# The first microseconds of a planned kernel: who loads the small table, who clears the state matrices, when the function table is loaded, and how long the zero products are

## The chip, the cores and the metric

The kernel runs on one core of one Trainium2 chip. A core has TensorE (PE, matmuls, with a separate record PEld for loading the stationary operand), VectorE (DVE), ScalarE (ACT), GpSimd (POOL) and SyncE (SP), which only issues transfers; 16 DMA engines move the data. The engines run their own instruction streams and meet at semaphores. The metric is device time in microseconds. Before the change it was 640.88 us, the median of three runs (640.83 to 641.22).

## The reference

A decay attention (linear attention with a decay per head) is followed by a feed-forward layer with a squared ReLU. All inputs are float32: q, k, v of 4 x 8 x 768 x 64 (batch, heads, positions, head size), one decay `lam` per head between 0.97 and 0.99, weights `w_in` 512 x 2048 and `w_out` 2048 x 512.

```python
for b in range(nb):                                  # blocks of 64 positions
    intra = np.einsum('bhic,bhjc->bhij', qb, kb) * Dmask[None]      # lam ** (i - j), i >= j
    intra = np.einsum('bhij,bhjd->bhid', intra, vb)
    inter = np.einsum('bhid,bhde->bhie', qb * lam_pow[None], kv_state)
    out[:, :, sl] = intra + inter
    kv_state = lam_block[None, :, None, None] * kv_state + np.einsum('bhsd,bhse->bhde', kb_dec, vb)
x = attn_out.transpose(0, 2, 1, 3).reshape(B * S, H * D)            # 3072 x 512
h = np.maximum(x @ w_in, 0.0)
return h * h @ w_out
```

## The kernel before

**The work.** Positions are cut into chunks of 128, six for each of the four batches; eight tiles of three chunks (384 rows) go through the feed-forward layer, which takes 16 steps per tile, one per 128 columns of `w_in`. A step is twelve matmuls into `h` (L507: the weights and the activations are each split into a high and a low part, and three of the four products are kept), the squared ReLU on ScalarE and VectorE, and nine matmuls into three output banks (L513, L514, L516). The attention of a chunk is done in two units of four heads. Nine chunks, those needed first, go through `unit_plain` (L302) in plain float32, the other fifteen through `unit_split` with operands in two parts.

**A plain unit.** SyncE loads one operand tile `pnt` of 512 KB (L311; four buffers). TensorE makes the scores of the four heads (L317); VectorE multiplies them with the mask (L322). ScalarE weights the values with the decay powers `wdec` (L328, four instructions). TensorE makes the state's update from the weighted values (L340), ScalarE scales it with `lc` into the next state (L356; for plain successors into the diagonal blocks of `diag`, whose other blocks must be zero), and TensorE adds up the values (L366 for the old state, L369 for the scores). VectorE multiplies with `rdec` (L372), and ScalarE and VectorE split the result into the two parts of `x` (L375, L376). `rdec` is made once: `wdec` is spread out by VectorE (L254), turned by TensorE with a flipped identity (L251) and scaled by VectorE (L258).

**The tables.** `start_tables` (L221) loads the 6 KB `lamx` (the decays, in two layouts) through SyncE's queue, clears `zero` (the matrix that the zero products read, which later serves as an output buffer), makes the position and chunk exponents, the flipped identity and the mask, clears the four `diag` buffers on POOL (L233), and raises the decays to their powers on POOL (L235 for `wdec`, L236 for `lc`). The function table of ScalarE is not loaded by a line of its own: it stands before the first ACTIVATE that the program has, that of L328.

**The order.** The order of all instructions on all engines is written out by a planner. Each operation has an engine, an estimated duration in us, a key (lower goes first), operations it depends on, and buffers. `order` (L77) keeps one clock per engine and takes, again and again, the operation that can start earliest; among those of an engine that can start at about the same time the lowest key wins. The estimate for a finished load is its duration plus 2.0 us, for POOL's work its duration plus 0.12. A matmul planned before `PE_SLOW` counts double. Where TensorE has a gap in the plan before `FILL_END` (45 us) and an output bank is free, the planner puts in products of zeros (`filler`, L238) that take `FILL` us each (double before `PE_SLOW`). The instructions are then emitted in that order; on the chip each engine runs its own in this order and waits where its data or its buffer isn't ready. The planner's clock has no other influence on the chip. The first operation, `start_tables`, is planned on POOL with 1.2 us; loads of tiles and weights depend on it in the plan (`o_start`), and the weighting of values depends on `o_pow`, 3.0 us on POOL behind it.

Of the kernel before, what the change touches and what calls it, by code (L numbers as in the profile page):

```python
# [19 lines left out]
P = 128  # L20
# [21 lines left out]
PLAIN, SPLIT = CHUNKS[:N_PLAIN], CHUNKS[N_PLAIN:]  # L42
# [17 lines left out]
class Plan:  # L60
# [13 lines left out]
        self.ops.append(o)  # L74
        return o

    def order(self, pe_slow, fill):  # L77

        need, out = {}, {}
        for o in self.ops:  # L80
            both = set(map(id, o.deps)) | set(map(id, o.after))
            need[id(o)] = len(both)
            for d in both:
                out.setdefault(d, []).append(o)
        ready = {e: [o for o in self.ops if o.eng == e and not need[id(o)]] for e in self.LAT}
        free = dict.fromkeys(self.LAT, 0.0)
        slots = {k: [(0.0, i) for i in range(n)] for k, n in self.slots.items()}
        done, filled, early = [], 0, sum(o.early is True for o in self.ops)
        while any(ready.values()):
            best = None  # L90
            for e, ops in ready.items():
                can = []
                for o in ops:
                    t = max([free[e]] + [d.end + d.lat for d in o.deps])
                    want = {}
                    for b in o.bufs:
                        if b.slot is None:
                            want[b.kind] = want.get(b.kind, 0) + 1
                    ok = o.early is not False or not early
                    for k, n in want.items():  # L100
                        if len(slots[k]) < n:
                            ok = False
                            break
                        t = max(t, sorted(slots[k])[n - 1][0] + 0.15)
                    if ok:
                        can.append((t, o))
                if not can:
                    continue
                soon = max(free[e], min(t for t, _ in can)) + 0.05
                t, o = min(((t, o) for t, o in can if t <= soon), key=lambda x: (x[1].key, x[0]))  # L110
                if best is None or t < best[0]:
                    best = (t, o)
            assert best is not None, "no operation can get its buffers"
            t, o = best
            if o.eng == "PE" and t < fill:

                while free["PE"] + (long := FILL * (2.0 if free["PE"] < pe_slow else 1.0)) < t:
                    bank = min(slots["bank"], default=(t, 0))
                    if bank[0] > free["PE"]:
                        break  # L120
                    done.append(Op("PE", long, 0, lambda i=bank[1]: self.filler(i), [], [], [], 0, None))
                    done[-1].start, done[-1].end = free["PE"], free["PE"] + long
                    free["PE"] += long
                    filled += 1
            dur = o.dur * (2.0 if o.eng == "PE" and t < pe_slow else 1.0)
            o.start, o.end = t, t + dur
            free[o.eng] = o.end
            for b in o.bufs:
                if b.slot is None:
                    slots[b.kind].sort()  # L130
                    b.slot = slots[b.kind].pop(0)[1]
                b.left -= 1
                b.end = max(b.end, o.end + o.lat)
                if not b.left:
                    slots[b.kind].append((b.end, b.slot))
            ready[o.eng].remove(o)
            done.append(o)
            early -= o.early is True
            for d in out.get(id(o), ()):
                need[id(d)] -= 1  # L140
                if not need[id(d)]:
                    ready[d.eng].append(d)
        assert len(done) - filled == len(self.ops), "operations need each other"
        return done
# [10 lines left out]

FIRST, SLOW_STEP, LAG, BEGIN2, SECOND, STEP, PE_SLOW, FILL_END, FILL = 18.0, 6.5, 16, 9.0, 1.5, 4.8, 7.0, 45.0, 0.43

BEHIND = 12  # L160

# [4 lines left out]
def kernel(ctx: ExitStack, tc: tile.TileContext, pn, pk, lamx, w, out):  # L166
    nc = tc.nc
# [3 lines left out]
    plan = Plan()  # L171
# [12 lines left out]
    tiles = {}  # L184
# [10 lines left out]
    flip, zero = tiles["g"][-1][:, 0:P], tiles["ob"][-1]  # L195
    lam, ej, ec = (tiles["g"][-1][:, P + 16 * i:P + 16 * i + n] for i, n in enumerate((H + NP, H, NP)))
# [20 lines left out]
    def at(b):  # L217
        return tiles[b.kind][b.slot]


    def start_tables():  # L221
        nc.sync.dma_start(out=lam, in_=lamx)
        nc.vector.memset(zero, 0.0)
        nc.gpsimd.iota(ej, pattern=[[0, H]], base=MID, channel_multiplier=-1, allow_small_or_imprecise_dtypes=True)
        nc.vector.memset(ec, float(C))

        nc.vector.memset(flip, 1.0)
        nc.vector.memset(mask, 1.0)
        nc.gpsimd.affine_select(out=flip, in_=flip, pattern=[[1, P]], compare_op=ALU.is_equal, fill=0.0, base=1 - P, channel_multiplier=1)
        nc.gpsimd.affine_select(out=mask, in_=mask, pattern=[[1, P]], compare_op=ALU.is_ge, fill=0.0, base=0, channel_multiplier=-1)  # L230

        for d in tiles["diag0"] + tiles["diag1"]:
            nc.gpsimd.memset(d, 0.0)  # L233

        nc.gpsimd.tensor_tensor(out=wdec, in0=lam[:, 0:H], in1=ej, op=ALU.pow)  # L235
        nc.gpsimd.tensor_tensor(out=lc, in0=lam[:, H:H + NP], in1=ec, op=ALU.pow)  # L236

    def filler(i):  # L238
        nc.tensor.matmul(tiles["bank"][i][:, 0:2 * P], zero[:, 0:P], zero[:, P:3 * P], start=True, stop=True)

    plan.filler = filler

    o_start = plan.op("POOL", 1.2, -99, start_tables, early=True)


# [3 lines left out]
    def turned():  # L249
# [9 lines left out]
        out=rdec, in0=at(rps).rearrange("p (n i) -> p n i", n=NP), in1=lam[:, H:H + NP].unsqueeze(2).broadcast_to([P, NP, C]), op=ALU.mult),  # L259
# [33 lines left out]
    def in_turn(name, o):  # L293

        if turn.get(name):
            o.after.append(turn[name])
        turn[name] = o
        return o
# [3 lines left out]
    def unit_plain(b, c, q, x, col, key, behind=None):  # L302

        prs = slice(2 * q, 2 * q + 2)
        t, s1, vd, xr = Buf("pnt"), Buf("s1"), Buf("vd"), Buf("xr")

        def add(eng, dur, dk, fn, deps, bufs, name=None):
            o = plan.op(eng, dur, key + dk, fn, deps, bufs, early=True)
            return in_turn(name, o) if name else o

        load = add("SP", 1.7, -8, lambda: nc.sync.dma_start(out=at(t), in_=pn[PLAIN.index((b, c)), q]), [o_start, behind], [t], "load")  # L311
        sc = [Buf("bank"), Buf("bank")]

        def scores():
# [5 lines left out]
        if (b, c, q) == (0, 0, 0):  # L320
            o_turned.after.append(o)
        so = [add("DVE", 0.36, 0, lambda h=h: nc.vector.tensor_tensor(  # L322
            out=at(s1).rearrange("p (n h) i -> p n h i", h=2)[:, :, h], in0=at(sc[h])[:, 0:2 * C].rearrange("p (n i) -> p n i", n=2),
# [38 lines left out]
        def values():  # L362
# [10 lines left out]
            out=at(xr), in0=at(y)[:, 0:2 * C].rearrange("p (n i) -> p n i", n=2), in1=rdec[:, prs], op=ALU.mult), [o, o_rdec], [y, xr], "xr")  # L373
# [3 lines left out]
            out=at(x)[1][:, prs, cs], in0=at(xr), in1=at(x)[0][:, prs, cs], op=ALU.subtract), [oh], [xr, x])  # L377
# [175 lines left out]
    begin = [FIRST, FIRST + LAG * SLOW_STEP]  # L553
# [5 lines left out]
    for f in range(NF):  # L559
        t = FIRST + f * SLOW_STEP  # L560
        ws.append((weights(f, 0, t - 7), weights(f, 1, t - 2)))
    for ti, cs in enumerate(TILES):
        x = Buf("x")
        ready = []
        n = len(cs) * NQ
        for j, (b, c) in enumerate(cs):
            for q in range(NQ):
                i = j * NQ + q
                if ti == 0:
                    ready += unit_plain(b, c, q, x, j * C, i * 1.5)  # L570
                elif ti == 1:
                    ready += unit_plain(b, c, q, x, j * C, BEGIN2 + i * SECOND)
                elif (b, c) in PLAIN:
                    ready += unit_plain(b, c, q, x, j * C, begin[ti - 1] + (1 + i / n * 11) * per[ti - 1], steps[0, BEHIND])
                else:

                    f0 = 0.5 if ti > 2 else 1.0
                    ready += unit_split(b, c, q, x, j * C, begin[ti - 1] + (f0 + i / n * (13 - f0)) * per[ti - 1], 4.0)
        os_ = [Buf("bank") for _ in cs]
        for f in range(NF):  # L580
            ffn(ti, f, x, ready, ws[f], os_, begin[ti] + f * per[ti])


    done = plan.order(PE_SLOW, FILL_END)
    opened = False
    n_early = sum(o.early is True for o in done)
    with tc.manual_schedule():
# [50 lines left out]
```

## Time and profile before

| | us |
|---|---|
| median of three runs | 640.88 |
| lowest and highest | 640.83, 641.22 |
| the profiled execution | 641.31 |
| its span, first to last instruction | 639.6 |
| TensorE busy in the span | 631.4 |
| VectorE busy | 469.4 |
| ScalarE busy | 372.1 |
| POOL busy | 5.5 |
| matmuls that ended the chain: L507, share of the span | 41% |
| the same for L513, L514 and L516, each | 14% |

Times in the trace are counted from the start of the span. "PE L317 x8" is eight records: each matmul of plain float32 operands stands there twice, so that the four matmuls of the scores make eight records. A row such as "5.50 0.71 PE L317 MATMUL ..." gives start, length, engine, line, operation, output and inputs, and in brackets how long the engine had been idle and what released it. SPq is SyncE's own stream of transfer issues. TensorE was granted its full clock share through the whole profile. A matmul's end is modelled, so starts are surer than lengths.

### The profile page before, as it was taken

Reading aid. Unit: us, or ns where it says so; the run is one execution under the profiler, and the core shown is the slowest. Engines: PE = TensorE matmul, PEld = TensorE weight load, DVE = VectorE, ACT = ScalarE, POOL = GpSimd, SP = SyncE. Lnnn points to the kernel's source line nnn. Section 1 sums busy time; section 2 is a strip of 40 time slices with the busy share of each in tenths; the row PEclk is TensorE's granted clock in tenths of the full one; section 3 lists DMA queues with packets and bytes.
Section 4 is the critical chain, followed back from the end, with each engine's and each line's share of the span. In section 5 each row is a group of like instructions: output and inputs, shape, how many; then the busy total and the mean of one; then the engine's idle time right before and its main releaser. Section 6 shows DMA issues by size and latency. Waiting matters only on the chain.

```text
span 639.6 us, 9612 instructions
## 1 busy us (share of the span) xinstructions
PE 631.4 (99%) x3620; PEld 569.4 (89%) x3620; DVE 469.4 (73%) x1046; ACT 372.1 (58%) x863; POOL 5.5 (1%) x15
## 2 busy tenths in 40 slices
PE   8999999999999999999999999999999999999997
PEld 6789989988899999999999999899899999999996
DVE  4999999934538998589975999769995799742222
ACT  6996777746535666367654657556674567532221
POOL 2000000000000000000000000000000000000000
PEclk9999999999999999999999999999999999999999
DMA  7725546521221220221202122121120121010001
GB/s 282 279 99 168 194 168 206 186 84 34 99 94 55 71 90 38 99 100 49 99 2 98 61 89 98 50 100 49 50 100 33 67 100 50 1 50 1 0 1 49
DMA packets 15165, 56.71 MB, mean 89 GB/s; under 512 B 1808, under 2 KB 1808, under 8 KB 15120
## 3 DMA queue, kind: packets, MB, share of 16 engines
q1 hardware_dynamic: 15120, 56.11, 24.8%
q8 instruction: 28, 0.46, 0.3%
q14 instruction: 17, 0.14, 0.1%
HBM read 49.81 MB, written 6.29 MB: 88 GB/s over the span
## 4 chain that ended last, share of the span: by engine, by line
PE 93%; ACT 3%; DMA 2%; issue 0%; DVE 0%; SPq 0%; ACTq 0%
PE h L507 41%; PE bank L516 14%; PE bank L513 14%; PE bank L514 14%; PE bank L473 2%; PE bank L430 2%; PE bank L472 2%; PE bank L450 2%; DMA pnt<-pn 2%; DMA pkt<-pk 1%; PE bank L317 1%; PE bank L369 1%; ACT vd L328 1%; ACT diag L356 1%; PE bank L340 0%
## 5 line engine op out<-in xcount | busy, mean ns | idle before, releaser
L513 PE MATMUL bank<-woh,gh 128*128 128x512 f32 x384 | 151.1, 394 | 0.7 <-ACT gh L524 0.7
L514 PE MATMUL bank<-wol,gh 128*128 128x512 f32 x384 | 150.7, 392 | 0.0
L521 ACT ACTIVATE g<-h 128x384 f32<-128x384 f32 x128 | 62.9, 492 | 139.3 <-PE h L507 138.9
L507 PE MATMUL h<-xh,wih 128*128 128x384 f32 x512 | 110.5, 337 | 0.0
L516 PE MATMUL bank<-woh,gl 128*128 128x512 f32 x384 | 110.4, 396 | 0.0
L507 PE MATMUL h<-xl,wih 128*128 128x384 f32 x512 | 109.8, 335 | 0.0
L507 PE MATMUL h<-xh,wil 128*128 128x384 f32 x512 | 109.4, 334 | 0.0
L527 DVE TENSOR_TENSOR g<-g 128x384 f32<-128x384 f32 x96 | 53.4, 557 | 75.7 <-ACT gh L526 75.2
L507 PEld LDWEIGHTS h<-xh,wih 128*128 128x128 f32 x512 | 89.8, 188 | 4.0
L507 PEld LDWEIGHTS h<-xl,wih 128*128 128x128 f32 x512 | 91.5, 188 | 0.0
L507 PEld LDWEIGHTS h<-xh,wil 128*128 128x128 f32 x512 | 90.6, 188 | 0.0
L516 PEld LDWEIGHTS bank<-woh,gl 128*128 128x128 f32 x384 | 70.0, 188 | 16.8 <-DVE gl L528 2.7
L513 PEld LDWEIGHTS bank<-woh,gh 128*128 128x128 f32 x384 | 72.1, 188 | 14.3 <-ACT gh L524 1.1
L514 PEld LDWEIGHTS bank<-wol,gh 128*128 128x128 f32 x384 | 72.2, 188 | 12.5
L528 DVE TENSOR_TENSOR gl<-g,gh 128x384 fp32r<-128x384 f32 x128 | 71.1, 556 | 14.5 <-ACT gh L524 11.1
L526 ACT ACTIVATE gh<-g 128x384 fp32r<-128x384 f32 x96 | 50.5, 526 | 2.5
L479 ACT COPY z<-bank 128x256 f32<-128x256 f32 x60 | 22.3, 372 | 36.8 <-PE bank L473 34.2
L480 DVE TENSOR_TENSOR z<-bank,z 128x256 f32<-128x256 f32 x60 | 25.0, 423 | 14.2 <-ACT z L479 13.0
L473 PE MATMUL bank<-pp,vv 128*128 128x256 f32 x120 | 29.9, 282 | 0.0
L472 PE MATMUL bank<-ab,ss 128*128 128x256 f32 x120 | 29.8, 281 | 0.0
L437 ACT COPY s<-bank 128x256 f32<-128x256 f32 x60 | 19.6, 374 | 12.0 <-PE bank L430 11.8
L485 DVE TENSOR_TENSOR xr<-z,zl 64x256 f32<-64x256 f32 x60 | 25.1, 418 | 2.0 <-ACT zl L481 1.0
(78 smaller groups left out, 774.8 us busy)
## 6 DMA issues: line engine op xcount, KB each, us to landing
pkt<-pk SPq DMA_DIRECT2D x30, 768.0 KB, 4.3
st<-w SPq DMA_DIRECT2D x32, 512.0 KB, 3.4
pnt<-pn SPq DMA_DIRECT2D x18, 512.0 KB, 5.0
out<-ob SPq DMA_DIRECT2D x23, 256.0 KB, 2.1
out<-z SPq DMA_DIRECT2D x1, 256.0 KB, 2.0
g<-lamx SPq DMA_DIRECT2D x1, 6.0 KB, 1.8
```

Source lines behind the costliest of these rows:

```text
L472: nc.tensor.matmul(y4[:, n], at(ss)[:, n, h].rearrange("p t d -> p (t d)"), at(ab)[:, i], start=n == 0, stop=False, skip_group_check=True)
L473: nc.tensor.matmul(y4[:, n], at(vv)[:, i].rearrange("p t d -> p (t d)"), at(pp)[:, i], start=False, stop=True, skip_group_check=True)
L480: zo.append(add("DVE", 0.36, 2, lambda h=h, part=part: nc.vector.tensor_tensor(out=at(z)[:, h], in0=part(0), in1=at(z)[:, h], op=ALU.add), ...
L485: nc.vector.tensor_tensor(out=at(xr)[half(h)], in0=at(z)[0:64, h], in1=at(zl)[:, h], op=ALU.add)
L507: nc.tensor.matmul(at(h)[:, 0:N], wt[:, cc, :], xt[:, cc, :], start=k == 0, stop=k == 3 * NCC - 1)
L513: nc.tensor.matmul(at(os_[j]), at(gh)[:, sl], woh[f], start=f == 0, stop=False)
L514: nc.tensor.matmul(at(os_[j]), at(gh)[:, sl], wol[f], start=False, stop=False)
L516: nc.tensor.matmul(at(os_[j]), at(gl)[:, sl], woh[f], start=False, stop=f == NF - 1)
L521: orr = plan.op("ACT", 0.45, key, lambda: nc.scalar.activation(at(g), at(h)[:, 0:N], AF.Relu), [o1], [h, g])
L526: ogh = plan.op("ACT", 0.47, key, lambda: nc.scalar.activation(at(gh), at(g), AF.Square), [orr], [g, gh])
L527: og = plan.op("DVE", 0.48, key, lambda: nc.vector.tensor_tensor(out=at(g), in0=at(g), in1=at(g), op=ALU.mult), [orr, ogh], [g])
L528: ogl = plan.op("DVE", 0.48, key, lambda: nc.vector.tensor_tensor(out=at(gl), in0=at(g), in1=at(gh), op=ALU.subtract), [og, ogh], [g, gh, gl])
```

## The change

`lamx` is issued from ScalarE's queue in place of SyncE's. The four `diag` buffers are cleared by VectorE in place of POOL. A ScalarE product of four columns of zeros is written to a place in the `g` buffer that nothing reads, which makes it the first ACTIVATE of the program. The zero products have 128 columns in place of 256. In the plan, `FILL` is halved to fit, the engines' clocks start at 1.45 (TensorE), 0.75 (SyncE) and 2.9 us (ScalarE) in place of 0, `PE_SLOW` is 4.9 in place of 7.0, and the loads of plain units no longer depend on `start_tables` (those of the weights and of the split units still do).

```diff
-    def order(self, pe_slow, fill):
+    def order(self, pe_slow, fill, begin):
...
-        free = dict.fromkeys(self.LAT, 0.0)
+        free = dict(dict.fromkeys(self.LAT, 0.0), **begin)
...
-FIRST, SLOW_STEP, LAG, BEGIN2, SECOND, STEP, PE_SLOW, FILL_END, FILL = 18.0, 6.5, 16, 9.0, 1.5, 4.8, 7.0, 45.0, 0.43
+FIRST, SLOW_STEP, LAG, BEGIN2, SECOND, STEP, PE_SLOW, FILL_END, FILL = 18.0, 6.5, 16, 9.0, 1.5, 4.8, 4.9, 45.0, 0.215
...
     def start_tables():
-        nc.sync.dma_start(out=lam, in_=lamx)
+        nc.scalar.dma_start(out=lam, in_=lamx)
...
         for d in tiles["diag0"] + tiles["diag1"]:
-            nc.gpsimd.memset(d, 0.0)
+            nc.vector.memset(d, 0.0)
+
+        nc.scalar.mul(tiles["g"][-1][:, P + 48:P + 52], zero[:, 0:4], 1.0)
...
     def filler(i):
-        nc.tensor.matmul(tiles["bank"][i][:, 0:2 * P], zero[:, 0:P], zero[:, P:3 * P], start=True, stop=True)
+        nc.tensor.matmul(tiles["bank"][i][:, 0:P], zero[:, 0:P], zero[:, P:2 * P], start=True, stop=True)
...
-        load = add("SP", 1.7, -8, lambda: nc.sync.dma_start(out=at(t), in_=pn[PLAIN.index((b, c)), q]), [o_start, behind], [t], "load")
+        load = add("SP", 1.7, -8, lambda: nc.sync.dma_start(out=at(t), in_=pn[PLAIN.index((b, c)), q]), [behind], [t], "load")
...
-    done = plan.order(PE_SLOW, FILL_END)
+    done = plan.order(PE_SLOW, FILL_END, {"PE": 1.45, "SP": 0.75, "ACT": 2.9})
```

## The prediction

> **What bounds the kernel now.** I read the page's head first, then the table of busy time by stage, then who waited for whom on TensorE, and last the first microseconds instruction by instruction.
>
> ```profile
> span 639.6 us, 9612 instructions
> PE 631.4 (99%) x3620; PEld 569.4 (89%) x3620; DVE 469.4 (73%) x1046; ACT 372.1 (58%) x863; POOL 5.5 (1%) x15
> ```
>
> ```profile
> core 0: us, PE busy (x) PEld busy (x) DVE busy (x) ACT busy (x) POOL busy (x), PEclk, DMA share, GB/s
> 5.50:12.00 6.50, 6.26 (x73) 4.97 (x72) 3.62 (x10) 5.68 (x20) 0.32 (x1) 1.00 0.97 383
> 12.00:18.00 6.00, 5.64 (x67) 4.13 (x65) 4.44 (x14) 5.91 (x22) 0.00 (x0) 1.00 0.62 209
> 18.00:24.00 6.00, 5.57 (x62) 4.20 (x62) 6.00 (x16) 5.94 (x25) 0.00 (x0) 1.00 0.95 361
> 24.00:36.00 12.00, 11.02 (x123) 8.93 (x124) 10.91 (x30) 10.60 (x35) 0.00 (x0) 1.00 0.58 203
> 36.00:100.00 64.00, 64.00 (x328) 57.97 (x329) 62.56 (x126) 48.73 (x97) 0.00 (x0) 1.00 0.47 159
> 100.00:636.00 536.00, 534.99 (x2968) 486.19 (x2966) 380.36 (x851) 294.55 (x671) 1.06 (x2) 1.00 0.19 68
> ```
>
> Each row is a stretch, its length, then each engine's busy time. From 36 us on TensorE is busy for 64.00 of 64 and 534.99 of 536 us. Up to there ScalarE is the fullest: 5.91 of 6 us from 12 to 18, 5.94 of 6 from 18 to 24. So the time is a start-up of 36 us, which ScalarE and what it waits for set, and a body that TensorE sets and this change hardly touches. A start-up that comes through earlier as a whole shortens the run by as much. The chain of waits (start, length) shows how it begins:
>
> ```profile
> 1.24 3.45 DMA pnt<-pn
> 4.76 1.28 ACT L328
> 6.06 0.36 ACT vd L328
> 6.46 1.04 PE bank L340 x8
> ```
>
> The first operand tile is under way from 1.24 to 4.69, then ScalarE loads its function table for 1.28 us, and only at 6.06 does it start its first useful work, the weighted values (L328), which TensorE's L340 needs. The instructions of the same stretch, and one far behind it that ends the start-up (start, length, engine, line):
>
> ```profile
> 0.80 0.39 SPq L222 DMA_DIRECT2D g<-lamx  x1
> 0.97 0.48 DVE L223 MEMSET ob<- 128x512 f32 x1 [0.97 <-PEq L631]
> 1.41 0.06 DVE L225 MEMSET g<- 128x4 f32 x1
> 1.45 0.17 DVE L227 MEMSET g<- 128x128 f32 x1
> 1.59 0.17 DVE L228 MEMSET mask<- 128x128 f32 x1
> 1.52 4.06 PE L239 MATMUL bank<-ob 128*128 128x256 f32 x10 [1.52 <-DVE ob L223]
> 1.94 0.29 POOL L230 TENSOR_SCALAR_AFFINE_SELECT mask<-mask 128x128 f32<-128x128 f32 x1
> 2.17 1.06 POOL L233 MEMSET diag<- 128x256 f32 x4
> 3.21 1.64 POOL L235 TENSOR_TENSOR wdec<-g 128x8 f32<-128x8 f32 x1
> 4.81 1.01 POOL L236 TENSOR_TENSOR lc<-g 128x4 f32<-128x4 f32 x1
> 4.88 0.43 DVE L254 COPY m<-wdec 128x512 f32<-128x512 f32 x1 [3.13 <-POOL wdec L235]
> 5.50 0.71 PE L317 MATMUL bank<-pnt 64*128 64x128 f32 x8
> 7.98 1.26 ACT L356 ACTIVATE diag<-bank,lc 64x64 f32<-64x64 f32 x4
> 36.89 0.50 PE L513 MATMUL bank<-woh,gh 128*128 128x512 f32 x1
> ```
>
> Three things end together here: the table load (6.04), the decay powers wdec on POOL (4.85), and the zero products, which hold TensorE until 5.50 although the tile has been there since 4.69.
>
> **The change part by part.** *The small table leaves SyncE's queue.* Its issue took 0.39 us at 0.80, and the first pnt issue came at 1.24. That issue now goes at 0.80, 0.44 us earlier, and the same 3.45 us later the tile is there: 4.25. Tiles two to four move by the same 0.44. The small table is issued by ScalarE instead, which had nothing to do before 4.76, so the 0.39 us of issue lies free. The first load also loses its planned dependence on the tables, which changes its place in the order only; it read none of them.
>
> *When the small table lands* is the unknown. Alone it took
>
> ```profile
> g<-lamx SPq DMA_DIRECT2D x1, 6.0 KB, 1.8
> ```
>
> 1.8 us from issue, so 2.6 at 0.80. Now it shares the engines with the tile from its first byte. Lower bound 2.6. Upper bound 4.25, landing with the tile.
>
> ```profile
> 1.80:2.00 0.20, 0.20 (x1) 0.20 (x1) 0.00 (x0) 0.00 (x0) 0.20 (x2) 1.00 0.38 19
> 2.20:2.40 0.20, 0.20 (x2) 0.20 (x1) 0.00 (x0) 0.00 (x0) 0.20 (x2) 1.00 0.53 165
> ```
>
> (Last columns: share of the DMA engines, GB/s.) Its bytes moved from about 1.8 to 2.2 at 19 GB/s; the tile's first bytes followed at 2.2 with half of the engines' time. I take ScalarE's issue at 0.9, as VectorE began at 0.97 and SyncE at 0.80, and let the 0.4 us of movement double for the sharing: 0.9 + 1.8 + 0.4 = 3.1, nearer the row of the same transfer than the tile's landing.
>
> [...] No row of this case shows two queues at work together; before, all loads went through one.
>
> *State matrices cleared by VectorE.* Off POOL: four clears, 2.17 to 3.21, 1.04 us. POOL is then free at 2.23 (1.94 + 0.29). On VectorE: the 512-wide clear and the 128-wide one lie 0.44 (0.97 to 1.41) and 0.14 us (1.45 to 1.59) from the next start, so 256 wide is some 0.25, four are 1.0, from 1.76 to 2.8. VectorE's next work was at 4.88, which hides it; without that cover it would cost 1.0. If clears and POOL's two selects hinder each other, the selects end at 3.3 at the latest, close to the 3.1 that POOL waits for anyway.
>
> So wdec starts at max(2.23, 3.1) + 0.05 = 3.15 instead of 3.21 and ends, 1.64 later, at 4.79. By the lower bound it is 2.65 and 4.29, by the upper 4.30 and 5.94. lc follows 1.01 later, at 5.8, 5.3 or 6.95; its first user, the state scaling, ran at 7.98, 1.9 us after the first weighting.
>
> *Function table at once.* One more ScalarE instruction, a 128x4 product, waits for the zeros (0.97 + 0.48 = 1.45). The table load stands before it: 1.5 + 1.28 = 2.8, and the product itself at most 0.36 (the 128x64 one of L328): 3.2. Nothing else stands on ScalarE until the tile lands at 4.25, so this is free and removes 1.28 from the chain. Late next is wdec.
>
> *Half-length zero products.* The planner started them at 0 and let the first load end at 1.32 + 1.7 + 2.0 = 5.02; five of 0.86 fitted, the ten matmul records of the row (two for each product). Now TensorE starts at 1.45, the load ends at 0.75 + 1.7 + 2.0 = 4.45, and (4.45 - 1.45) / 0.43 gives six, twelve records.
>
> ```profile
> 4.24 0.91 PE L239 MATMUL bank<-ob 128*128 128x256 f32 x2
> 4.66 0.91 PE L239 MATMUL bank<-ob 128*128 128x256 f32 x3
> 4.98 0.60 PE L239 MATMUL bank<-ob 128*128 128x256 f32 x2
> 5.20 0.38 PE L239 MATMUL bank<-ob 128*128 128x256 f32 x1
> ```
>
> (First column: starts.) They stood 0.42 us apart up to 4.66 and 0.22 from 4.98: TensorE doubled its speed at about 4.85. Half as long, twelve times 0.21 from 1.52, and 0.15 for the first, end at 4.2: the scores (L317) start at 4.3 instead of 5.50. They took 0.71 us at full speed. Of that, 0.28 is done by 4.85 at half speed, so they end at about 5.3 instead of 6.21: 0.9 earlier, and still ahead of the weighting's end.
>
> *Sum.* The first weighting waits for the tile (4.25), the function table (3.2) and wdec (4.79), and starts at 4.84 instead of 6.06: 1.2 us earlier. By the bounds it is 4.34 (1.7 earlier) or 5.99 (0.1 earlier). The profiled execution took 641.31 us, 639.6 of it span; 1.2 off makes 640.1. It lies 0.43 above the median of the runs, 640.88, so in the median's terms 1.2 less is 639.7.
>
> *The order written out afterwards.* All later work is emitted in the order that the planner's clock gives, and that clock now runs some 0.6 us earlier with full speed from 4.9 instead of 7.0. Keys and durations are the same, so I expect nearly the same order, but any swap up to 36 us can gain or cost. What it could gain are the waits of TensorE from 5.5 to 37 us:
>
> ```profile
> PE bank L366 <- ACT diag L356: 0.9, 2, 0.7
> PE bank L340 <- ACT vd L328: 0.4, 2, 0.2
> PE bank L317 <- DMA pnt<-pn: 0.4, 1, 0.4
> ```
>
> What it could cost lies in the zero products: the planner puts them into any gap up to 45 us, before only into gaps of 0.43, now of 0.215.
>
> ```profile
> L239 PE MATMUL bank<-ob x12: 379/634/793, 1.5 to 18.3; 128*128 128x256 f32 x12
> 17.98 0.70 PE L239 MATMUL bank<-ob 128*128 128x256 f32 x2
> ```
>
> Of the twelve records ten were at the start and two at 17.98: a single product went into a later gap. I take nothing for it, since the count of gaps between 0.215 and 0.43 is not shown; bounds are 0 and a dozen, 2.6 us.
>
> **The rivals.**
> - *Full cover.* The small table is not held up and wdec ends at 4.29: the weighting starts at 4.34, 1.7 earlier, 639.2. For it: the table is 6 KB beside 512. Against: tile and table start together.
> - *The small table lands with the tile.* Each engine alternates between the two queues, and the 4.25 us bound holds: wdec at 5.94, the weighting at 5.99, 0.1 to 0.2 earlier, 640.7. Here the change doesn't do what it says.
> - *The loads decide.* They come only 0.44 us earlier, and from 5.5 to 12 us the DMA engines are full (0.97). If the following tiles set the pace, the gain ends there: 640.4. Against it: TensorE waited for a tile only 0.4 us in this whole stretch.
> - *The new order also closes waits.* Tile and state waits, 0.4 + 0.9 = 1.3 on top of 1.2: 638.4.
> - *Slower: zero products in the start-up's small gaps.* Each holds TensorE for 0.215 us and takes a bank whose reader must be done, and TensorE works in order. Where a gap of the plan isn't one on the chip, what follows is late. It decides from the sixth uncovered one (6 x 0.215 = 1.3 against 1.2 gained); a dozen give 640.88 - 1.2 + 2.6 = 642.3. For it: TensorE's idle time from 5.5 to 36 is 0.24 + 0.36 + 0.43 + 0.98 = 2.0 us, so most stretches have no hole. Against it: one in 32 us before.
>
> **How the numbers follow.** A measurement of this kernel can tell about 0.2% (1.3 us) from no change: under 639.6 is faster, over 642.2 slower. The forecast, 639.7 with 639.2 to 640.2 of its own, has 0.32, of which 0.10 falls under 639.6; full cover 0.19, the table held back 0.10, the loads 0.08, the waits closed 0.15, the zero products 0.16, of which 0.13 is over 642.2. Faster: 0.19 + 0.15 + 0.10 = 0.44. Same: 0.22 + 0.10 + 0.08 + 0.03 = 0.43. Slower 0.13. The range goes from 638.4, where the waits are closed, to 642.0, short of the dozen zero products.
>
> **What would show it.** The first pnt issue near 0.80; the table load on ScalarE near 1.5; POOL's wdec starting near 3.15 (2.65 in full cover, 4.3 if held back); the scores near 4.3 and the weighting near 4.84; twelve short zero products ending near 4.2; then TensorE's first second-layer product (L513, at 36.89 before) some 1.2 us earlier, and every count of TensorE's matmuls as before but for L239. If wdec is early but L513 isn't, the order or the loads took the gain; if L239 shows many more than the first twelve, the slower rival is at work. The prediction is wrong if ScalarE's early start doesn't reach 36 us.

## The result and the profile after

The changed kernel takes 645.28 us (median; 644.44 to 646.05), the kernel before, run beside it, 640.86: a ratio of 1.0067 with a 95% interval of 1.0053 to 1.0080. It is 4.4 us slower, and the forecast of 639.7 with its range of 638.4 to 642.0 is wrong. In the changed kernel every line behind the clears (L233) has a number two higher than before (L507 is now L509, L513 is L515).

The page's head of the changed kernel; its profiled execution took 645.06 us:

```profile
span 643.3 us, 9671 instructions
PE 633.4 (98%) x3652; PEld 572.6 (89%) x3652; DVE 470.1 (73%) x1050; ACT 372.5 (58%) x864; POOL 4.7 (1%) x11
```

The span grew by 3.7 us. TensorE has 32 records more (3652 against 3620): its zero products, 44 records in place of 12. Two records are one product, so six products stand at the start and 16 later. The table by stage:

```profile
5.50:12.00 6.50, 5.33 (x44) 4.23 (x44) 2.50 (x6) 4.21 (x16) 1.85 (x2) 1.00 0.78 296
12.00:18.00 6.00, 5.58 (x70) 4.15 (x70) 4.54 (x14) 5.36 (x19) 0.00 (x0) 1.00 0.65 235
18.00:24.00 6.00, 6.00 (x78) 5.12 (x80) 6.00 (x17) 5.96 (x24) 0.00 (x0) 1.00 0.87 266
24.00:36.00 12.00, 11.04 (x132) 9.41 (x130) 10.88 (x31) 11.33 (x39) 0.00 (x0) 1.00 0.66 236
36.00:40.00 4.00, 3.03 (x35) 2.65 (x33) 3.91 (x10) 3.89 (x11) 0.00 (x0) 1.00 0.12 23
100.00:636.00 536.00, 534.99 (x2969) 486.48 (x2968) 379.25 (x849) 295.56 (x674) 1.21 (x2) 1.00 0.19 67
```

From 100 us on TensorE is as full as before (534.99 of 536). From 36 to 40 us, where it had no idle time before, it is busy for 3.03 of 4, and 2.05 of that are eight of the 16 late zero products, as the rows below show. The first microseconds, instruction by instruction (start, length, engine, line):

```profile
0.80 0.41 ACTq L222 DMA_DIRECT2D g<-lamx  x1
0.80 1.80 SPq L313 DMA_DIRECT2D pnt<-pn  x4
1.23 1.28 ACT L235 ACT_TABLE_LOAD   x1 [1.23 <-PEq L633]
1.52 2.93 PE L241 MATMUL bank<-ob 128*128 128x128 f32 x12 [1.52 <-DVE ob L223]
1.76 1.09 DVE L233 MEMSET diag<- 128x256 f32 x4
4.41 1.23 PE L319 MATMUL bank<-pnt 64*128 64x128 f32 x8
4.73 1.64 POOL L237 TENSOR_TENSOR wdec<-g 128x8 f32<-128x8 f32 x1 [2.50 <-DMA g<-lamx]
6.40 2.02 ACT L330 ACTIVATE vd<-pnt,wdec 128x64 f32<-128x64 f32 x8 [3.67 <-POOL wdec L237]
6.80 1.19 PE L342 MATMUL bank<-vd,pnt 128*64 128x64 f32 x8 [1.17 <-ACT vd L330]
7.93 1.23 PE L319 MATMUL bank<-pnt 64*128 64x128 f32 x8
11.82 0.71 PE L319 MATMUL bank<-pnt 64*128 64x128 f32 x8
```

Table load, clears, first tile and twelve zero products stand where they were forecast. Two things do not. POOL waits for the small table until 4.73, so the first weighting starts at 6.40, 0.34 later than before. And TensorE is still at half speed at 7.93 (1.23 for the scores that took 0.71 at 5.50 before); the spacing of its matmuls halves at about 10.2, and 0.71 is back at 11.82. Then, on TensorE and ScalarE, where the start-up ends; the first row is the kernel before, the others are the changed one:

```profile
24.28 0.96 PE L507 MATMUL h<-xh,wih 128*128 128x384 f32 x4
33.41 0.98 PE L509 MATMUL h<-xh,wih 128*128 128x384 f32 x4
36.65 0.40 PE L342 MATMUL bank<-vd,pnt 128*64 128x64 f32 x8
36.98 2.05 PE L241 MATMUL bank<-ob 128*128 128x128 f32 x16
40.13 0.50 PE L515 MATMUL bank<-woh,gh 128*128 128x512 f32 x1 [1.10 <-ACT gh L526]
37.23 0.69 ACT L279 ACTIVATE m<-st 128x512 f32<-128x512 f32 x1
37.82 0.48 ACT L523 ACTIVATE g<-h 128x384 f32<-128x384 f32 x1
39.57 0.51 ACT L526 CAST gh<-g 128x384 fp32r<-128x384 f32 x1
```

The first feed-forward step (L509) starts at 33.41 in place of 24.28: the planner put it behind the scores of twelve units, where nine stood ahead of it before. The matmuls of the attention that stand ahead of the second-layer product are done at 36.98, and from there to 40.13, 3.15 us, TensorE has only zero products (2.05) and a wait (1.10) for the squares `gh`, which ScalarE reaches at 39.57. Who waited for whom, 5 to 640 us:

```profile
PE bank L515 <- ACT gh L526: 1.8, 3, 1.1
PE bank L319 <- DMA pnt<-pn: 1.3, 2, 1.0
PE bank L342 <- ACT vd L330: 1.2, 1, 1.2
PE h L509 <- ACT wih L288: 0.3, 1, 0.3
```

Of the waits of before (`diag`, `vd`, `pnt`: 0.9, 0.4, 0.4) the first is gone and the other two have grown. The wait for `gh` was 0.7 before, all of it behind 100 us; the 1.1 us at 40 us is new. VectorE and ScalarE are both nearly full from 36 to 40 us (3.91 and 3.89 of 4). The chain of waits begins with another transfer:

```profile
0.80 3.79 DMA g<-lamx
```

The small table, and not the tile, is what the start now waits for.

To compare whole runs I use a *lost time* worked out from the traces: the time reached, less the matmuls started by then, each at the median distance between the starts of its kind in the kernel before; zero products count as nothing. At 36 us it is 12.05 before and 12.35 after, at 40 us 12.0 and 15.1, at the end 16.6 and 20.6. The end is the start of the last matmul; there the two profiled executions are 4.0 us apart (their spans 3.7). Of these 4.0 us 0.3 are lost up to 36, 2.8 from 36 to 40, and 0.9 later; some 0.5 of the 0.9 at 117 us, where TensorE waits 0.27 us for weights (`wih`) that ScalarE writes.

### The profile page after: what moved, and what is told of

Read it like the earlier page. It is cut to its first block, busy times and chain, and to the rows that moved or that the text cites. A ratio compares the mean times of both kernels' runs of the same rounds, so it can differ in the third digit from the quotient of the medians.

```text
span 643.3 us, 9671 instructions
## 1 busy us (share of the span) xinstructions
PE 633.4 (98%) x3652; PEld 572.6 (89%) x3652; DVE 470.1 (73%) x1050; ACT 372.5 (58%) x864; POOL 4.7 (1%) x11
## 4 chain that ended last, share of the span: by engine, by line
PE 89%; DMA 4%; ACT 3%; DVE 2%; issue 0%; POOL 0%; SPq 0%; ACTq 0%; DVEq 0%; POOLq 0%
PE h L509 38%; PE bank L518 13%; PE bank L515 13%; PE bank L516 13%; PE bank L475 2%; PE bank L474 2%; PE bank L432 2%; DMA pkt<-pk 2%; PE bank L452 2%; PE bank L319 1%; PE bank L371 1%; DMA pnt<-pn 1%; DMA st<-w 1%; DMA g<-lamx 1%; ACT m L279 1%; ACT vd L330 0%
## 5 line engine op out<-in xcount | busy, mean ns | idle before, releaser
L515 PE MATMUL bank<-woh,gh 128*128 128x512 f32 x384 | 151.2, 394 | 1.8 <-ACT gh L526 1.8
L509 PE MATMUL h<-xh,wih 128*128 128x384 f32 x512 | 110.6, 337 | 0.3 <-ACT wih L288 0.3
L509 PE MATMUL h<-xl,wih 128*128 128x384 f32 x512 | 109.8, 335 | 0.0
L509 PE MATMUL h<-xh,wil 128*128 128x384 f32 x512 | 109.4, 334 | 0.0
L509 PEld LDWEIGHTS h<-xh,wih 128*128 128x128 f32 x512 | 89.8, 188 | 4.7 <-ACT wih L288 0.6
L509 PEld LDWEIGHTS h<-xl,wih 128*128 128x128 f32 x512 | 91.5, 188 | 0.0
L509 PEld LDWEIGHTS h<-xh,wil 128*128 128x128 f32 x512 | 90.6, 188 | 0.0
L515 PEld LDWEIGHTS bank<-woh,gh 128*128 128x128 f32 x384 | 72.1, 188 | 15.6 <-ACT gh L526 2.7
L482 DVE TENSOR_TENSOR z<-bank,z 128x256 f32<-128x256 f32 x60 | 24.8, 422 | 12.8 <-ACT z L481 11.7
```

The costliest lines, as they stand in the source:

```text
L482: zo.append(add("DVE", 0.36, 2, lambda h=h, part=part: nc.vector.tensor_tensor(out=at(z)[:, h], in0=part(0), in1=at(z)[:, h], op=ALU.add), ...
L509: nc.tensor.matmul(at(h)[:, 0:N], wt[:, cc, :], xt[:, cc, :], start=k == 0, stop=k == 3 * NCC - 1)
L515: nc.tensor.matmul(at(os_[j]), at(gh)[:, sl], woh[f], start=f == 0, stop=False)
```

## The experiments

Names in capitals in the expectations are theories. START: what the chip does differently in the first microseconds costs the time. ORDER: the re-planned order does. SHARING: the small table lands late because the tile's load runs beside it. ZEROS: the 16 late zero products cost it. STEP: the late place of the first feed-forward step does. CLOCK: TensorE reaches full speed late, or loses it again. QUEUE: ScalarE's queue is slow in itself. Lost time is that of the profiled execution, which in e5, e7 and e15 is 1 to 2 us off the median.

| run | median us | ratio to before, 95% | profiled us | lost at 36 | at 40 | at end |
|---|---|---|---|---|---|---|
| before | 640.86 | 1 | 641.31 | 12.0 | 12.0 | 16.6 |
| after | 645.28 | 1.0053 to 1.0080 | 645.06 | 12.4 | 15.1 | 20.6 |
| e1 start alone | 641.01 | 0.9990 to 1.0007 | 641.14 | 12.1 | 12.2 | 16.7 |
| e2 order alone | 644.93 | 1.0044 to 1.0071 | 644.93 | 13.7 | 15.1 | 20.5 |
| e3 table back | 643.20 | 1.0024 to 1.0044 | 643.24 | 11.1 | 13.3 | 18.8 |
| e4 two parts | 640.58 | 0.9983 to 1.0000 | 640.58 | 11.1 | 11.4 | 15.9 |
| e5 PE_SLOW back | 644.98 | 1.0045 to 1.0072 | 642.98 | 11.9 | 11.8 | 18.5 |
| e6 no late zeros | 645.20 | 1.0052 to 1.0076 | 645.66 | 12.1 | 14.9 | 21.2 |
| e7 both back | 643.56 | 1.0026 to 1.0050 | 642.49 | 10.4 | 10.3 | 17.8 |
| e8 hole filled | 644.45 | 1.0038 to 1.0062 | 644.45 | 11.1 | 14.0 | 19.7 |
| e9 short start | 640.67 | 0.9985 to 1.0003 | 640.14 | 10.9 | 11.0 | 15.4 |
| e10 e5, full zeros | 644.77 | 1.0038 to 1.0064 | 644.80 | 11.7 | 11.8 | 20.3 |
| e11 step forward | 647.43 | 1.0083 to 1.0110 | 647.83 | 14.2 | 16.1 | 23.4 |
| e12 tile later | 642.82 | one run | 642.82 | 11.1 | 12.4 | 18.1 |
| e13 step back | 643.58 | 1.0024 to 1.0050 | 643.58 | 13.7 | 14.4 | 18.9 |
| e14 e11, no zeros | 646.06 | 1.0066 to 1.0090 | 646.06 | 13.7 | 14.0 | 21.6 |
| e15 e14, table back | 644.83 | 1.0039 to 1.0070 | 645.87 | 13.8 | 15.3 | 21.4 |

**Start or order: e1 and e2.** e1 is the kernel before with the three edits of the first microseconds that are on the chip and not in the zero products (the table's queue, the clears, the early function table); its order and its full zero products are those of before.

```diff
-        nc.sync.dma_start(out=lam, in_=lamx)
+        nc.scalar.dma_start(out=lam, in_=lamx)
...
-            nc.gpsimd.memset(d, 0.0)
+            nc.vector.memset(d, 0.0)
+
+        nc.scalar.mul(tiles["g"][-1][:, P + 48:P + 52], zero[:, 0:4], 1.0)
```

> The order, the planner's numbers and the 256-wide zero products of before, with only the four edits of the start that the chip sees: the small table from ScalarE's queue, VectorE's clears, the early table load. Two theories of the 4.4 us that the change lost. ORDER (the new order of loads, zero products and units costs it): this run stays within 1 us of before, 640.2 to 641.6, because the only loss left is wdec, 0.3 us late. START (small table landing with the tile, and a TensorE clock that opens late after short zero products, cost it): 642 or more, with wdec on POOL at 4.7 and the first scores at half speed.

e2 is the opposite: the changed kernel with these lines as they were before.

> The order of the changed kernel with its half-length zero products, and the start of before: small table first on SyncE's queue, POOL clears, table load behind the tile. ORDER: 643 to 645.5, nearly all of the loss. START: near before, 640.5 to 641.5, since the small table lands at 2.6 again. If TensorE's clock opens late here too (scores of the second unit 1.23 us instead of 0.71), that part of START belongs to the short zero products and not to the small table.

e1 takes what the kernel before takes (ratio 0.9998), although its small table is late too, the power on POOL starting at

```profile
4.84 1.64 POOL L237 TENSOR_TENSOR wdec<-g 128x8 f32<-128x8 f32 x1 [2.61 <-DMA g<-lamx]
37.01 0.50 PE L515 MATMUL bank<-woh,gh 128*128 128x512 f32 x1
```

4.84, 1.63 later than before, and its second-layer product at 37.01 is within 0.12 of before. e2 gives back 0.35 of the 4.4 us. START, taken alone, falls, and ORDER holds. One thing stays mixed in e2: it keeps the half-length zero products, its scores still take 1.23 us at 7.54 and 1.07 at 12.81, and 1.6 us more than before are lost by 36 us. e9, further down, has half-length zero products in the old order and is level with the kernel before. In e2 TensorE runs dry at the same work:

```profile
38.28 2.05 PE L239 MATMUL bank<-ob 128*128 128x128 f32 x16
40.92 0.50 PE L513 MATMUL bank<-woh,gh 128*128 128x512 f32 x1 [0.59 <-ACT gh L524]
```

It has 2.64 us there without useful work.

**The small table: e3 and e12.** e3 is the changed kernel with the one line back on SyncE's queue, ahead of the first tile.

```diff
-        nc.scalar.dma_start(out=lam, in_=lamx)
+        nc.sync.dma_start(out=lam, in_=lamx)
```

> The changed kernel with one line undone: the small table goes first on SyncE's queue again, everything else and the whole order as changed. wdec then starts near 2.7 and ends near 4.3, the first weighting starts near 4.8 when the tile lands. START: 640 to 641.5, as the weighting is 1.6 us earlier than in the changed kernel and TensorE's hole from 5.6 to 6.8 closes. ORDER: 642.5 to 644.5, at most the 1.5 us by which the first units ran late come back.

e12 keeps it on ScalarE's queue, but puts a second copy of the table, to a place that nothing reads, ahead of the tile on SyncE's queue, so that the tile is issued 0.44 later. It adds that one load.

```diff
         nc.scalar.dma_start(out=lam, in_=lamx)
+        nc.sync.dma_start(out=tiles["g"][-1][:, P + 64:P + 64 + H + NP], in_=lamx)
```

> The changed kernel with one more small load ahead of the tiles on SyncE's queue (a second copy of the small table to a place that nothing reads), so that the first tile is issued at 1.24 again while the small table still goes through ScalarE's queue at 0.80. Theory SHARING (small table and tile take turns on the DMA engines): the small table lands at 2.6 to 3.0, not 4.6. Theory QUEUE (ScalarE's queue itself is slow): 4.6 as in the changed kernel. Only the landing counts here.

The transfer in the changed kernel (bytes of each, then the us from issue to landing):

```profile
g<-lamx ACTq DMA_DIRECT2D x1, 6.0 KB, 3.8
```

and the same transfer, from the same queue, in e12:

```profile
g<-lamx ACTq DMA_DIRECT2D x1, 6.0 KB, 1.8
```

SHARING holds: beside the tile's load the 6 KB take 2.0 us longer, and it is not the queue, only what runs with it. e3 brings 2.1 us back, e12 (a single run) 2.5. But the dry stretch stays: lost time in e3 goes from 11.1 at 36 us to 13.3 at 40. Its start-up arrives 1.2 us before the one of the changed kernel, and it is still 0.34% slower than before, as ORDER had it (642.5 to 644.5).

**The late zero products: e6.** The changed kernel with its 16 zero products behind the first six left out, the order otherwise the same.

```diff
-                    done.append(Op("PE", long, 0, lambda i=bank[1]: self.filler(i), [], [], [], 0, None))
+                    done.append(Op("PE", long, 0, (lambda i=bank[1]: self.filler(i)) if filled < 6 else lambda: None, [], [], [], 0, None))
```

> The changed kernel with its order kept and the sixteen zero products after the start left out (they write banks that nobody reads). ZEROS: 641 to 642.5, each cost 0.2 us. STEP: they lie in real holes, so nothing comes back: 644.3 to 645.8, within 0.5 us of the changed kernel, and TensorE idles from 37 to 40 us.

Nothing comes back (645.20), and up to 40 us the lost time is that of the changed kernel (14.9 against 15.1), so ZEROS falls. On TensorE:

```profile
39.91 0.50 PE L515 MATMUL bank<-woh,gh 128*128 128x512 f32 x1 [3.13 <-ACT gh L526]
```

and, from the table by stage,

```profile
40.00:45.00 5.00, 5.00 (x17) 4.28 (x18) 4.95 (x11) 2.36 (x6) 0.00 (x0) 0.66 0.47 179
```

What was 2.05 of zero products and 1.10 of waiting is now 3.13 of waiting: these eight stood in a hole that was there anyway. And behind the empty hole TensorE's granted clock is 0.66 on the mean of 5 us (0.50 for 3.4 of them).

**The late full speed: e8.** e8 is the changed kernel with six more zero products behind the first scores, where TensorE had waited 1.17 us.

```diff
+            if (b, c, q) == (0, 0, 0):
+                for _ in range(6):
+                    filler(5)
```

> The changed kernel with six more half-length zero products directly behind the first scores, where TensorE idled from 5.6 to 6.8 waiting for the weighted values. Theory CLOCK (that hole keeps TensorE at half speed until about 9.9 us, which costs over 1 us): the second unit's scores take 0.71 us instead of 1.23, and the time falls to 643.5 to 644.5 with less scatter. If the hole has nothing to do with it, 645.0 to 646.

TensorE is at full speed from 5.9 us on in place of 10.2, and at 36 us e8 has lost 1.2 us less than the changed kernel (11.1). At 40 us 1.1 of it is left (14.0), at the end 0.9 (19.7). The median is 0.8 lower, but the runs of the two overlap (643.79 to 645.44 against 644.44 to 646.05). So the late full speed is some 0.8 of the 4.4 us, and not shown beyond the scatter. Nor does the hole decide it alone: e5, below, starts on the chip as the changed kernel does, with the same wait of 1.17 us, and its second scores take 0.71 us at 7.90.

**The planner's slow time: e5, e7 and e10.** e5 is the changed kernel with `PE_SLOW` at 7.0 again; that alone puts the first step behind nine units again (at 25.79 us in e5). e7 also has the table on SyncE's queue. e10 is e5 with five full-length zero products at the start.

```diff
-... PE_SLOW, FILL_END, FILL = 18.0, 6.5, 16, 9.0, 1.5, 4.8, 4.9, 45.0, 0.215
+... PE_SLOW, FILL_END, FILL = 18.0, 6.5, 16, 9.0, 1.5, 4.8, 7.0, 45.0, 0.215
```

> The changed kernel with one number of the planner undone: full TensorE speed is planned from 7.0 us again instead of 4.9. The start on the chip stays as changed; in the order that comes out, the first feed-forward step stands behind nine units' scores again instead of twelve, and five zero products follow after the start instead of sixteen. Theory STEP (the new order puts the first step last, so its squares come late and TensorE runs dry when the units are used up): 640.5 to 641.7, almost the whole loss is back. Theory ZEROS (the late zero products hold TensorE): the same direction, by a third of them left, 642 to 643. Neither, but the late small table and clock: 644 or more.

> Two lines undone: the small table goes first on SyncE's queue, and full speed is planned from 7.0. VectorE's clears, the early table load and the short zero products stay. If the two losses add up (small table and clock 2, order 3 or more), this is the fastest so far: 639.2 to 640.2, with the scores at 4.7 and the weighting at 4.8. If an early start is lost on the way to 36 us: 640.5 to 641.2.

> The kernel of the run with 7.0 put back, with five full-length zero products at the start in place of six half-length ones, all else the same. Theory CLOCK (the half-length ones end at 4.2, the hole behind them and the one before the first update leave TensorE at half speed for one or two periods of 3.4 us more, differently in each execution): the median falls from 645 to 642.5 to 643.3 and the scatter from 3.3 to under 1 us; the wait at 167 us (1.9 us) stays. If the clock is not behind the scatter: 644.5 to 645.5, scatter as before.

At 40 us the loss is gone in all three: 11.8, 10.3 and 11.8, against 12.0 before. Yet they take 644.98, 643.56 and 644.77: e5 misses what STEP asked for, and e7 both of its ranges. Part of it stands 130 us later, in e7:

```profile
169.84 0.98 PE L509 MATMUL h<-xh,wih 128*128 128x384 f32 x4 [1.94 <-ACT g L523]
```

TensorE waits 1.9 us for a first ScalarE operation of a step; the kernel before waits there for 0.5 us at most, for `gh`. In e10 it costs more, since the clock is lowered behind it:

```profile
170.00:175.00 5.00, 3.93 (x15) 3.74 (x16) 3.65 (x10) 4.84 (x12) 0.00 (x0) 0.76 0.01 3
175.00:180.00 5.00, 5.00 (x21) 3.99 (x21) 0.56 (x1) 0.73 (x2) 0.00 (x0) 0.89 0.00 0
```

From 160 to 180 us e10 loses 4.0 us (13.7 to 17.7), e5 2.4, e7 2.1, the kernel before 0.9. The mean granted clock of each run goes with this. e10's two runs at 0.999 and 1.000 take 643.2, its three at 0.997 take 644.8 to 645.6; half speed for 3.4 of 643 us would give 0.997. In e5 the profiled run, 642.98, has 1.000 and the slowest, 646.33, has 0.994, but one of 645.08 has 0.999, so the clock is not all of its scatter. What CLOCK forecast for e10, a scatter under 1 us, did not come: full products at the start did not keep the clock from falling at 170 us.

**The step's place: e11, e13, e14 and e15.** e11 is the changed kernel with the five operations of the first step moved forward to where their inputs are planned to be ready; nothing else is moved.

```diff
+    done = [o for o in done if o not in first]
+    at_ = 1 + max(done.index(d) for d in first[0].deps)
+    done.insert(at_, first[0])
+    for o, skip in zip(first[1:], (4, 3, 1, 0)):
...
```

> The changed kernel with its own order, in which only the first feed-forward step (its twelve matmuls and its four operations on ScalarE and VectorE) is emitted as soon as all that it depends on has been emitted, nine places earlier. Theory STEP (TensorE runs dry at 37 to 40 because that step's squares come last): the hole at 37 to 40 closes, 642.8 to 643.8, about 2 us less than the changed kernel; the rest, clock and small table, stays. If it stays within 0.7 us of 645.3, STEP is wrong.

It got slower still, 647.43. Eight zero products still stood right ahead of the second-layer product (41.43 to 43.63 us), where there was now no hole to fill, and the clock was at 0.55 from 35 to 40 us:

```profile
35.00:40.00 5.00, 4.55 (x24) 3.55 (x24) 4.08 (x13) 4.30 (x14) 0.00 (x0) 0.55 0.01 3
```

That did not settle STEP. e13 brings the step's late place alone into the kernel before; e14 is e11 with the late zero products left out as in e6; e15 is e14 with the table on SyncE's queue.

```diff
+    o2 = next(i for i, o in enumerate(pe) if first[3] in o.deps)
+    for o, o_next in zip(first, (pe[o2 - 2], act[40], act[40], act[41])):
+        done.insert(done.index(o_next), o)
+    done.insert(done.index(first[3]) + 1, first[4])
```

> The kernel before, with one thing moved: the five operations of the first feed-forward step stand behind the last scores, as in the changed kernel, instead of behind nine units' scores. Start, zero products and all other order as before. The hole decides: TensorE waits for gh before its first second-layer product, which starts at about 39.4 instead of 36.9, and the run takes 643.0 to 643.6 us. Rival, the late opening of TensorE's clock decides and the hole costs nothing lasting: within 0.5 us of the kernel before.

> The changed kernel with the first feed-forward step moved forward, as in the run before of that kind, and its 16 late zero products left out. The hole decides: without the wait for gh and without zero products in front of it, the first second-layer product comes at about 38 and the run takes 642.5 to 643.5 us. Rival, the late opening and closing again of TensorE's clock decides: 645 to 647.

> As the run before, with the small table first on SyncE's queue again. If the two losses found so far, 2.1 us for the small table's place and 2 to 3 us for the hole, add up: 640.5 to 641.5 us, level with the kernel before. Rival, the order has further losses: 642 to 644.

e13 takes 643.58, 2.6 more than before, and its second-layer product comes at 39.23, both as expected. But the time does not go where it was expected. Who waited for whom:

```profile
PE bank L340 <- DVE xr L372: 1.4, 1, 1.4
PE bank L513 <- ACT gh L524: 1.1, 3, 0.5
```

and the table by stage:

```profile
25.00:30.00 5.00, 3.58 (x47) 2.81 (x46) 4.98 (x13) 2.99 (x10) 0.00 (x0) 1.00 0.90 327
30.00:35.00 5.00, 5.00 (x41) 4.25 (x42) 4.40 (x13) 4.85 (x17) 0.00 (x0) 0.66 0.27 85
```

Without the step's 2.3 us of matmuls at 24 to 26.6, TensorE runs out of work while VectorE is full (4.98 of 5); then its clock is at 0.66 on the mean of 5 us. The wait for `gh` is 0.5 at the longest. So the step's place does cost 2.6 us in an otherwise unchanged kernel, through the work that it takes away from TensorE there more than through the late squares. The lowered clock is part of this price: four of the five runs have a mean of 0.997, the fifth has 0.999 and takes 642.63.

e14 and e15 say that the reverse doesn't work. Of e14, who waited for whom:

```profile
PE bank L342 <- ACT vd L330: 2.5, 3, 1.2
PE h L509 <- ACT wih L288: 2.1, 2, 1.4
PE bank L515 <- ACT gh L526: 0.7, 2, 0.5
```

The wait for `gh` is down from 1.8 to 0.7, and two others have grown, for the weighted values and for the weights of steps, both ScalarE's work. 646.06 and 644.83 are not what the hole as single cause demanded (642.5 to 643.5, and 640.5 to 641.5). 646.06 lies in the range of the rival, but the clock that closes again is not what made it: in this very run the granted clock is 1.000. 644.83 lies outside both ranges of e15. The hole that is closed in this order comes back as other waits.

**What is left of the idea: e4 and e9.** e4 is the kernel before with the clears on VectorE and the early function table only (the second part of e1's diff). e9 also has fourteen records of half-length zero products at the start in place of ten full ones. Both keep the order of before to the instruction.

```diff
+    def filler(i, k):
+        n, times = (P, 2 if k < 2 else 1) if k < 5 else (2 * P, 1)
+        for _ in range(times):
+            nc.tensor.matmul(tiles["bank"][i][:, 0:n], zero[:, 0:P], zero[:, P:P + n], start=True, stop=True)
```

> The kernel before with only the two edits that were costed as free: VectorE clears the state matrices, ScalarE loads its function table at once; order, zero products and the small table's queue as before. Both theories: the weighting starts near 4.9 instead of 6.06, the scores still wait for the zero products until 5.50, so the state's update ends near 6.6 instead of 7.5: 0.5 to 1.2 us faster, 639.7 to 640.4, if an early start reaches 36 us. If it stays at 640.9, early starts are lost on the way.

> The order of before kept to the letter, with the early table load, VectorE's clears, the small table first on SyncE's queue, and seven half-length zero products at the start in place of five full ones, so that TensorE is free when the tile lands at 4.7. If an early start is kept all the way once the order is left alone: scores at 4.7, weighting at 4.8, the first second-layer product 1.3 to 1.7 us earlier than before, 639.2 to 639.7, faster than both kernels. If short products keep TensorE's clock shut, it scatters by 1.5 us or more and its median is over 640.3.

In the profiled executions the start-up does come through earlier: 0.9 and 1.2 us less lost at 36 us, still 0.7 and 1.2 at the end. In the medians it is 0.5 and 0.3 us, and both intervals reach 1.0: they scatter (639.81 to 641.19 and 639.56 to 642.37) more than the kernel before does. Neither can be told from it; nothing tried here beats it by 0.2%. For e9 this is what its rival said (a median over 640.3 and a scatter of 1.5 us or more); its scores still take 1.23 us at 4.81 and 0.82 at 6.59.

## Why the prediction was wrong

*The step that failed.* "Keys and durations are the same, so I expect nearly the same order." The planner compares its engines' clocks before it looks at keys, and `PE_SLOW` doubles durations up to a time. With 4.9 in place of 7.0 the first step's five operations went behind three more units, and with 7.0 alone put back (e5) they did not. e2 has that order and, but for the half-length zero products, nothing of the early start on the chip, and is 0.58% slower; e1 has the start and not the order, and is level; e9 has half-length products and not the order, and is level too. The text gave the order a sentence and a cost in zero products only. Of the waits that it had listed as possible gains the one for `diag` closed; those for `vd` and `pnt` grew, and the dry stretch at 37 us, 2.8 us of lost time, is a place that it did not look at. The small table's place costs 2.1 more in this order (e3) and nothing that can be told from the noise in the old one (e1). These prices overlap and do not make a sum.

*What bounds the start-up* was misread as well. "Up to there ScalarE is the fullest" holds from 12 to 18 us; in the same table VectorE is fuller from 18 to 24 (6.00 of 6 against 5.94) and TensorE and VectorE from 24 to 36 (11.02 and 10.91 against 10.60). An early weighting on ScalarE need not carry to 36 us where two other engines are as full; in e13 it is VectorE that TensorE waits for.

*The small table's landing* was mis-sized: 3.1 forecast, 4.25 as the upper bound, 4.6 measured (0.80 + 3.8). With it `wdec` started at 4.73 in place of 3.15 and the weighting at 6.40 in place of 4.84. The rival "lands with the tile" was right in mechanism, and even its bound was short by 0.35. In the changed kernel's trace 32 packets of SyncE's queue, 0.13 MB, start between 1.80 and 2.74 us and none of the small table; from 2.74 to 4.00 its 144 stand among 133 of SyncE's queue, nearly one for one. The landing took 3.8 us beside the tile's load against 1.8 when that is issued 0.44 later (e12). The forecast of 3.1 was an estimate from a transfer that had the tile's load 0.44 us behind it.

*The zero products* were placed right (twelve records, 1.52 to 4.2), but what they do to the speed was read wrongly. The text took 4.85, where the speed doubled before, as a fixed time. After shorter products and two holes (4.2 to 4.4, and 1.17 us ahead of 6.80) it doubled at about 10.2; in e8, with zero products in the second hole, at 5.9. e8 prices this at 1.2 us at 36 us, of which 0.9 is left at the end, in one profiled execution of each; e5 has the same holes and is at full speed at 7.90, so the holes alone do not decide it.

*The slower rival* had the side right and the mechanism wrong. There are 16 late zero products, more than its dozen, but e6 shows that nothing comes back without them; eight of them fill the hole at 37 us. The sign by which the text meant to recognise it, "many more than the first twelve" on that line, was there and misled: it is a sign that the planner saw gaps, not that the products made them.

*Right:* the first tile's issue at 0.80 and the scores at 4.41 (4.3 forecast); the function table off the chain (1.23 to 2.51, forecast 1.5 to 2.8); four clears on VectorE in 1.09 us (1.0), hidden. That "a start-up that comes through earlier as a whole shortens the run by as much" fits the profiled executions where the order is kept (e4, e9: 0.7 and 1.2 us at the end); in the medians it is 0.3 to 0.5 us, not beyond the noise.

*Open:* why the weights come late at 117 us in the changed kernel, and what e5 and e7 lose beside the wait at 170 us, is not settled. Nor is the part of the dropped dependence of the loads and of the engines' new starting times in the order, which no run changes alone. The share of the step's place in the changed kernel itself is open too: 2.6 us is its price in the kernel before, and moving it forward in the changed one (e11, e14) brought nothing back.

## What to carry to other kernels

Where a planner writes the order, a change of its clocks or its slow time can change the whole order: compare the two streams of instructions engine by engine before giving a price to the edit itself, and keep the old order if only the start is to be changed. A small load that gates the start did better here ahead of the large one on the same queue (1.6 to 1.8 us to land) than beside it on another (3.8 to 3.9). A zero product in a late place can show a hole (e6); ask what the engine lacks there.

## What the runs showed of the hardware

- A 6 KB load took 1.6 to 1.8 us ahead of a 512 KB load (e9, before) and 3.8 to 3.9 beside it on the other queue (the changed kernel, e1, e6, e10). On the other queue with the large load 0.44 us behind it took 1.8 (e12, one run).
- The start at half speed does not appear in the granted clock, which reads 1.00 from 5.5 to 12 us in the changed kernel while the scores take 1.23 in place of 0.71. The trace's first clock record begins at 10.20 there and at 4.86 in the kernel before, where the spacing of the zero products halves at 4.85; the view has 1.00 ahead of it all the same. In the five kernels with five full-length products at the start it begins at 4.9 to 6.7; with half-length ones it is 4.7 to 6.9 in seven profiles and 10.1 to 13.6 in five (one execution of each). The later closings do appear there (0.66 in e6 and e13, 0.55 in e11, 0.76 in e10).
- The clock fell behind holes: of 1.82 us in e10, 3.13 in e6, and in e13 one of 1.42 in a stretch where TensorE was busy for 3.58 of 5 us; in e11 behind two of 0.33 and 0.62 us. A hole of 1.94 us did not in e7's profile, where the granted clock stayed at 1.00 from 170 to 175 us. The same place in the program lost 2.1 us from 160 to 180 in e7 and 4.0 in e10.
- In the clock records, the ends of the runs left out, half speed lasts 3.41 us or twice that (e11, e15), and begins a whole number of 3.41 us behind the last opening: 49 of them in e10, 9 in e6, 7 in e11, e13 and e15. The fall at the end fits the same count: 186 in the kernel before (4.86 to 639.74), 185 in the changed one (10.20 to 641.67). In stretches counted this way the hole in e10 lies in one, and the one in e7 is divided, 0.96 and 0.97 us. Whether that is what decided, no run tests. Idle time alone does not decide: the clock fell behind a stretch with 0.95 us idle in e11 and not behind one with 1.59 in e5.
